# Group and mask columns of a neighborhood attention kernel, computed by GpSimd in the opening

## The chip, the core and the metric

The kernel runs on one core of a Trainium2 chip. The metric is device time in microseconds (us). Before the change, three runs took 326.32, 326.91 and 329.77 us, median 326.91. The engines are TensorE (PE in the profile, its weight loads PEld), VectorE (DVE), ScalarE (ACT), GpSimd (POOL) and SyncE (SP), which here only issues transfers.

## What is computed

A dilated neighborhood attention with one head on an image of 224 x 224 pixels and 192 channels. Each query attends to 7 x 7 keys, two pixels apart in both directions, in a window that is pushed inwards at the borders.

```python
qkv = x @ wqkv
q, k, v = qkv[..., :C], qkv[..., C:2 * C], qkv[..., 2 * C:]
r0 = clip(arange(H) - 6, 0, H - 13)
c0 = clip(arange(W) - 6, 0, W - 13)
ri = r0[:, None] + arange(7) * 2
ci = c0[:, None] + arange(7) * 2
...
logits = einsum('bnc,bnkc->bnk', q, k[nidx]) * C ** -0.5
p = softmax(logits, axis=-1)
o = einsum('bnk,bnkc->bnc', p, v[nidx]) @ wo
```

All arrays are bfloat16; `nidx` are the positions `ri * W + ci`.

## The kernel before

**Tiles and steps.** Since the dilation is 2, rows and columns of each parity are independent. The kernel works in 28 steps, each a row parity `rc` and a block `j` of 8 query rows of that parity, in an order written out by hand in `seq` (L508). A step has seven score groups (`s_group`, L397): per key tile `n` of 8 columns and column parity `cc`, two matmuls (L411 and L412) give the scores of 128 keys with up to 112 queries in PSUM, and ScalarE's Exp (L415) puts them into `p_sb`. The projections are folded into the weights: the query side `g = (scale * Wq Wk^T) x` is made by `g_piece` (L335) and `edge_item` (L287) from the transposed image `xt`, and the values are the plain image rows, with `Wv Wo` folded into `WP` (L265). `y_unit` (L417) multiplies `p_sb` with the values, `o_mm` (L440) applies `WP`, and `o_out` (L460) divides by the sum.

**The buffers that matter.** `XA` and `XB` hold the keys, `GA` and `GB` the query side. They have 192 channels in two parts; in `XB` and `GB` 64 of the 128 partitions are not needed for channels, and hold one-hot rows of the key's column and row (`onehots`, L191) against mask columns and mask rows (`masks`, L202): so the matmul L412 adds -30000 where a key lies outside the query's window. The mask columns are a copy of `cmE` (L187, written by VectorE from an iota of GpSimd); they are the same for all groups. There are six groups of `GB` buffers (`gorder`, L129), for row parity, block parity and border; `masks(eng, gi)` fills group `gi`, for both column parities unless one is named. `XN[rc]` holds the values: 14 tiles of 448 columns, of which the first 64 are the pattern `grp` (L155), written by `grp_copy` (L208) in two instructions (128x896, L209, and 128x64, L211), and 384 are loaded from the image (L104 and L110).

**What sets the order.** The schedule is manual: each engine works through its instructions in program order, and waits are put in where data depend on each other. What happens in the first two steps beside the score groups is written by hand in the table `early` (L532), by the number of the score group; later steps follow rules in the loop (L552). Masks of group 0 are written in the opening by VectorE (L214, L263), those of group 2 in entry 0 of `early`, of group 1 in entries 6 and 12, of groups 4, 3 and 5 in steps 2, 3 and 8 (L610). `grp_copy(0)` runs on ScalarE in the opening (L261), `grp_copy(1)` on ScalarE in entry 12 (L543).

**Queues.** SP issues the transposing loads of `xt` (L92), its half of the first value loads (L117) and the weights. GpSimd's program in the opening is: iotas (L134), three small memsets (L171 to L173), then the copy `gate` (L217), which reads one element of the second block of `xt` and so holds GpSimd until that part has landed; then seven value loads of `XN[0]` (L218), two copies of the one-hots by DMA (L195, in step 0), a second `gate` on `wo_hi` (L564), and the value loads of `XN[1]` and of the later steps (L104). Each transfer that GpSimd issues takes about 0.6 us of its time (L104: 595 ns).

Of the kernel before, what the change touches and what calls it, by code (L numbers as in the profile page):

```python
# [27 lines left out]
def kernel(  # L28
# [7 lines left out]
    nc = tc.nc  # L36
# [31 lines left out]
    GA, GB = {}, {}  # L68
# [7 lines left out]
    CROW = (slice(64, 96), slice(0, 32))  # L76
# [52 lines left out]
    gorder = [(0, 0, 1), (1, 0, 0), (0, 1, 0), (1, 1, 0), (0, 0, 0), (1, (NJ - 1) % 2, 1)]  # L129
# [49 lines left out]
    cmE = const.tile([128, S, BR], BF, name="cmE")  # L179
# [11 lines left out]
    def onehots(eng, cc, rc):  # L191
        c_, r_ = CROW[cc], RROW[cc]
        if rc == 1:
            both = slice(min(c_.start, r_.start), max(c_.stop, r_.stop))
            eng.dma_start(out=XB[cc][1][both], in_=XB[cc][0][both])  # L195
            return
        eng.tensor_copy(out=XB[cc][rc][c_].rearrange("p n (r c) -> p n r c", c=KC),
                        in_=t_c[c_].rearrange("p (n c) -> p n c", c=KC).unsqueeze(2).to_broadcast([32, NK, SLOTS, KC]))
        eng.tensor_copy(out=XB[cc][rc][r_],
                        in_=rowT[r_].rearrange("p r c -> p (r c)").unsqueeze(1).to_broadcast([32, NK, 128]))  # L200

    def masks(eng, gi, ccs=(0, 1)):  # L202
        for cc in ccs:
            g = GB[gorder[gi] + (cc,)]
            eng.tensor_copy(out=g[CROW[cc]], in_=cmE[CROW[cc]])
            eng.tensor_copy(out=g[RROW[cc]], in_=rm[RROW[cc], gi, :].unsqueeze(1).to_broadcast([32, S, BR]))

    def grp_copy(eng, rc):  # L208
        eng(out=XN[rc][:, 0:NK * XP].rearrange("p (n c) -> p n c", c=XP)[:, :, 0:64],  # L209
            in_=grp[:].unsqueeze(1).to_broadcast([128, NK, 64]))  # L210
        eng(out=XN[rc][:, NK * XP:], in_=grp[:])  # L211

    onehots(nc.vector, 0, 0)
    masks(nc.vector, 0, (0,))  # L214

    gate = const.tile([1, 1], BF, name="gate")
    nc.gpsimd.tensor_copy(out=gate[:], in_=xt[1][0:1, 0, 4, 0:1])  # L217
    load_both(nc.gpsimd, 0, (13, 11, 9, 7, 5, 3, 1))  # L218
# [29 lines left out]
    for nm, c, rows, o0, d0 in (("lo", 0, None, 0, 0), ("hi", 128, slice(0, 64), 128, 0), ("olo", -64, slice(64, 128), 0, 64), ("ohi", 64, None, 0, 0)):  # L248
# [7 lines left out]
        for dst, src in outs:  # L256
            if own:
                nc.vector.tensor_single_scalar(out=dst, in_=src, scalar=scale, op=ALU.mult)
            else:
                nc.scalar.mul(dst, src, scale)  # L260
    grp_copy(nc.scalar.copy, 0)  # L261
    onehots(nc.vector, 1, 0)
    masks(nc.vector, 0, (1,))  # L263

    def fold_wo():  # L265
# [113 lines left out]
    def slots(cc, n):  # L379

        lo, hi = KC * n, KC * n + QW
        if cc == 0:
            return [(lo, min(hi, S))]
        lo = max(lo, HALO)
        return [(lo, hi)] if hi <= S else [(lo, S), (0, hi - S)]
# [31 lines left out]
    def y_unit(st, cc, h, kt, eng, fill=0):  # L417
        h0, h1 = HS[h]
        kp = slice(0, 64 if st.first else 128)
        y = ps_y.tile([128, 512], F32, name="y", tag="y")  # L420
        for _ in range(fill):
            nc.tensor.matmul(y[:, 0:128], lhsT=ident[:], rhs=ident[:], start=True, stop=True)
        first = True
        for n in range(NK):
            if not any(max(lo, h0) < min(hi, h1) for lo, hi in slots(cc, n)):
                continue
            for (lo, hi, p, off) in st.p[(cc, n)]:
                a_, b_ = max(lo, h0), min(hi, h1)
                if a_ >= b_:
                    continue  # L430
                d = XP * n + ((128, 0), (256, 384))[cc][kt]
                nc.tensor.matmul(y[:, BR * (a_ - h0):BR * (b_ - h0)], lhsT=XN[st.rc][kp, d:d + 128],  # L432
                                 rhs=p[kp, off + BR * (a_ - lo):off + BR * (b_ - lo)],
                                 start=first, stop=True, skip_group_check=True)
                first = False
        i0, i1 = h0 // NO, h1 // NO
        o = st.ysb[cc][:, kt, :, :].rearrange("p n (i r) -> p i n r", r=BR)[:, i0:i1]
        eng(out=o, in_=y[:, 0:BR * (h1 - h0)].rearrange("p (i n r) -> p i n r", n=NO, r=BR))  # L438

    def o_mm(st, ns, ccs=(0, 1), home=None):  # L440

        if home is None:
            po = ps_go.tile([128, 4, 256], F32, name="po", tag="go")
        else:
            po = home[0].tile([128, 2, 256], F32, name="po" + home[1], tag=home[1])
        k = 0
        for n in ns:
            for cc in ccs:
                for kt in range(2):
                    nc.tensor.matmul(po[:, k, 0:C + 1], lhsT=st.ysb[cc][:, kt, n, :], rhs=WP[:, cc, kt, 0:C + 1],  # L450
                                     start=(kt == 0), stop=(kt == 1))
                k += 1
        rs = work.tile([128, 4, 1], F32, name="rs", tag="rs", bufs=4)
        nc.vector.reciprocal(out=rs[:, 0:k], in_=po[:, 0:k, C:C + 1])  # L454
        if st.o is None:
            st.o = work.tile([128, 2 * NO, C], BF, name="o_sb", tag="o_sb", bufs=4)
        t0, step = 2 * ns[0] + ccs[0], 3 - len(ccs)
        return po, rs, k, st.o[:, t0:t0 + step * (k - 1) + 1:step, :]

    def o_out(po, rs, k, o, act=False):  # L460
        if act:
            for i in range(k):
                nc.scalar.activation(out=o[:, i], in_=po[:, i, 0:C], func=ACTF.Copy, scale=rs[:, i])
            return
        nc.vector.tensor_tensor(out=o, in0=po[:, 0:k, 0:C], in1=rs[:, 0:k].to_broadcast([128, k, C]), op=ALU.mult)  # L465
# [46 lines left out]
    steps = []  # L512
# [13 lines left out]
    def run_y(now):  # L526
# [4 lines left out]

    early = {  # L532
        0: (lambda: masks(nc.vector, 2, (0,)), lambda: g_piece(0, 0, 2), lambda: key_copy(1, 0, 0, nc.scalar.copy, nc.vector.tensor_copy), lambda: key_copy(0, 0, 1, nc.vector.tensor_copy, nc.vector.tensor_copy), lambda: rest(nc.vector.tensor_copy), lambda: edge_item(0), lambda: masks(nc.vector, 2, (1,)),),
        2: (lambda: edge_copies(0, 0, nc.vector), lambda: g_piece(0, 1, 0),),
        3: (lambda: key_copy(0, 1, 1, nc.scalar.copy, nc.scalar.copy), lambda: g_piece(0, 1, 1, mid=nc.vector.tensor_copy, mid2=nc.vector.tensor_copy),),
# [4 lines left out]
        9: (lambda: y_unit(steps[0], 1, 0, 1, nc.scalar.copy), lambda: y_unit(steps[0], 1, 0, 0, nc.vector.tensor_copy),),  # L540
        10: (lambda: key_copy(1, 1, 1, nc.vector.tensor_copy, nc.vector.tensor_copy), lambda: fold_wo(), lambda: edge_copies(1, 0, nc.vector),),
        11: (lambda: o_out(*o_mm(steps[0], PIECES[0])), lambda: o_out(*o_mm(steps[0], PIECES[1])), lambda: y_unit(steps[1], 0, 0, 1, nc.scalar.copy), lambda: y_unit(steps[1], 0, 0, 0, nc.vector.tensor_copy),),
        12: (lambda: grp_copy(nc.scalar.copy, 1), lambda: masks(nc.vector, 1, (1,)), lambda: o_out(*o_mm(steps[0], PIECES[2])), lambda: y_unit(steps[1], 1, 1, 0, nc.scalar.copy),),  # L543
        13: (lambda: o_out(*o_mm(steps[0], PIECES[3])), lambda: y_unit(steps[1], 1, 1, 1, nc.scalar.copy),),
        14: (lambda: y_unit(steps[1], 1, 0, 1, nc.scalar.copy), lambda: y_unit(steps[1], 0, 1, 1, nc.vector.tensor_copy),),
        15: (lambda: y_unit(steps[1], 1, 0, 0, nc.vector.tensor_copy),),
# [4 lines left out]
    PIECES = ((0, 1), (2, 3), (4, 5), (6,))  # L551
# [129 lines left out]
```

## Time and profile before

| | us |
|---|---|
| median of three runs | 326.91 |
| profiled execution | 325.78 |
| its span, first to last instruction | 323.8 |
| TensorE busy | 306.1 (95%) |
| VectorE busy | 267.6 (83%) |
| ScalarE busy | 251.0 (78%) |
| GpSimd busy | 216.0 (67%) |

The mean granted TensorE clock is 0.993 of full speed. The profile is one execution, 325.78 us, which is 1.98 us more than its span. In a timeline a row gives the start in us, the duration, engine, line, operation, what is written from what, and the shape; in brackets stands the idle time of the engine before it and what ended that. In a group of instructions the two numbers after the bar are the busy time in us and the mean of one in ns. In a table of stretches the busy time of TensorE, its weight loads, VectorE, ScalarE and GpSimd follow each other.

### The profile page before, as it was taken

The numbers are of one execution on the slowest core, as the hardware profiler recorded it, in microseconds if no ns is written. First come the engines' busy times: TensorE is split into PE (matmuls) and PEld (weight loads), VectorE is DVE, ScalarE is ACT, GpSimd is POOL, SyncE is SP. The second block draws the span as 40 slices with busy tenths as digits, with TensorE's granted clock in tenths as the row PEclk, the third lists the DMA queues.
The fourth block names the chain that finished last, engine by engine and source line by source line (L and its number), as shares of the span: only waits on it lengthen the run. The fifth ranks groups of instructions, "written<-read, shape, count | busy, mean of one in ns | idle before, by whom it ended". The sixth has DMA issues, their size and how long they took to land.

```text
span 323.8 us, 12228 instructions
## 1 busy us (share of the span) xinstructions
PE 306.1 (95%) x4988; PEld 269.8 (83%) x4988; DVE 267.6 (83%) x533; ACT 251.0 (78%) x519; POOL 216.0 (67%) x445
## 2 busy tenths in 40 slices
PE   7689999998989999999999999999999999999981
PEld 6467987888879888988899888988899888988980
DVE  8968899987878989888988889888988898887771
ACT  5688767886868887878888798878787887888652
POOL 2144888797877766786667767679678786863053
PEclk9999999999999999999999999999999999999997
DMA  8999799999999999999998999899989943654233
GB/s 167 166 263 168 185 171 237 162 236 219 181 226 223 229 199 157 237 196 214 189 183 216 213 188 163 224 204 224 177 197 217 194 117 113 166 153 112 45 106 109
DMA packets 106109, 59.47 MB, mean 184 GB/s; under 512 B 92712, under 2 KB 100031, under 8 KB 106054
## 3 DMA queue, kind: packets, MB, share of 16 engines
q1 hardware_dynamic: 89270, 40.43, 64.6%
q0 software_dynamic: 16576, 18.13, 22.5%
q8 instruction: 39, 0.64, 0.9%
q10 hardware_dynamic: 208, 0.15, 0.2%
q14 instruction: 16, 0.13, 0.1%
HBM read 19.59 MB, written 19.27 MB: 120 GB/s over the span
## 4 chain that ended last, share of the span: by engine, by line
PE 54%; DMA 20%; DVE 7%; SPq 6%; POOL 5%; issue 4%; ACT 2%; POOLq 0%; DVEq 0%; ACTq 0%
DMA xn<-in_x_dram 16%; PE y L432 15%; PE po L450 12%; PE pg L354 10%; PE s_ps L411 7%; PE s_ps L412 7%; SPq L92 4%; DMA out_dram<-o_sb 4%; DVE o_sb L465 4%; POOL xn L104 3%; PE pg L362 3%; DVE ysb L438 2%; SPq L110 1%; POOL out_dram L608 1%; ACT ysb L438 1%
## 5 line engine op out<-in xcount | busy, mean ns | idle before, releaser
L104 POOL DMA_DIRECT2D xn<-in_x_dram x316 | 178.6, 595 | 58.6 <-DMA xn<-in_x_dram 24.9
L415 ACT ACTIVATE p_sb<-s_ps 128x448 bf16<-128x448 f32 (+3 forms) x196 | 105.4, 539 | 21.3 <-PE s_ps L412 20.7
L432 PE MATMUL y<-p_sb,xn 128*128 128x112 bf16 (+5 forms) x1736 | 107.3, 207 | 1.6 <-DMA xn<-in_x_dram 1.3
L432 PEld LDWEIGHTS <-xn 128*128 128x128 bf16 (+1 forms) x1736 | 94.8, 97 | 13.9 <-issue 5.4
L411 PE MATMUL s_ps<-ga,xa 128*128 128x112 bf16 (+4 forms) x812 | 98.1, 210 | 1.4 <-DVE xa L278 0.8
L412 PE MATMUL s_ps<-gb,xb 128*128 128x112 bf16 (+4 forms) x812 | 97.8, 210 | 0.1
L438 ACT CAST ysb<-y 128x504 bf16<-128x504 f32 (+1 forms) x137 | 71.6, 543 | 33.4 <-PE y L432 31.8
L465 DVE TENSOR_TENSOR o_sb<-po,rs 128x768 bf16<-128x768 f32 x109 | 93.6, 859 | 4.7
L450 PE MATMUL po<-WP,ysb 128*128 128x193 bf16 x770 | 82.6, 247 | 1.0 <-DVE ysb L438 0.5
L412 PEld LDWEIGHTS <-xb 128*128 128x128 bf16 (+1 forms) x812 | 75.8, 98 | 0.9 <-issue 0.6
L411 PEld LDWEIGHTS <-xa 128*128 128x128 bf16 (+1 forms) x812 | 72.6, 98 | 2.2 <-DVE xa L278 1.0
L450 PEld LDWEIGHTS <-ysb 128*128 128x128 bf16 x784 | 62.7, 98 | 2.9 <-ACT ysb L438 1.1
L354 PE MATMUL pg<-xt,wz 128*128 128x327 bf16 (+3 forms) x336 | 51.2, 288 | 1.7 <-DMA xt<-in_x_dram 1.6
L438 DVE CAST ysb<-y 128x392 bf16<-128x392 f32 (+1 forms) x87 | 51.7, 596 | 0.6 <-PE y L432 0.2
L454 DVE RECIPROCAL rs<-po 128x4 f32<-128x4 f32 x110 | 19.4, 177 | 23.2 <-PE po L450 21.7
L368 DVE CAST gb<-pg 64x872 bf16<-64x872 f32 x27 | 28.6, 1057 | 5.0 <-PE pg L362 3.6
L354 PEld LDWEIGHTS <-wz 128*128 128x128 bf16 x336 | 24.4, 98 | 9.8 <-DMA xt<-in_x_dram 1.9
L366 ACT CAST ga<-pg 128x872 bf16<-128x872 f32 x28 | 24.8, 884 | 8.4 <-PE pg L354 8.3
L371 DVE CAST gb<-pg 64x848 bf16<-64x848 f32 x28 | 29.2, 1044 | 0.4
L278 ACT COPY xa<-xt 128x896 bf16<-128x896 bf16 x28 | 26.3, 939 | 0.0
L376 ACT CAST ga<-pg 128x848 bf16<-128x848 f32 x28 | 24.2, 864 | 0.5 <-PE pg L354 0.3
L280 DVE COPY xb<-xt 64x896 bf16<-64x896 bf16 x54 | 21.4, 396 | 0.8
(93 smaller groups left out, 182.4 us busy)
## 6 DMA issues: line engine op xcount, KB each, us to landing
out_dram<-o_sb SPq DMA_DIRECT2D x25, 630.0 KB
xn<-in_x_dram POOLq DMA_DIRECT2D x316, 48.0 KB, 4.5
xn<-in_x_dram SPq DMA_DIRECT2D x38, 48.0 KB
xn<-in_x_dram SPq DMA_DIRECT2D x12, 96.0 KB
out_dram<-o_sb POOLq DMA_DIRECT2D x12, 78.8 KB, 4.2
xt<-in_x_dram SPq DMA_TRANSPOSE x56
out_dram<-o_sb SPq DMA_DIRECT2D x50, 9.0 KB
xn<-in_x_dram POOLq DMA_DIRECT2D x7, 96.0 KB, 3.9
```

The costliest lines, as they stand in the source:

```text
L104: eng.dma_start(out=XN[rc][p0:p0 + 64, XP * n + 64:XP * (n + 1)], in_=xp[r0:r0 + 15:2, KC * n:KC * (n + 1), :])
L278: ea(out=XA[rc][:, cc, :, k0:k0 + 64].rearrange("p n (r c) -> p r n c", c=KC), in_=t[:, 2 * cc, rc:16:2, :].rearrange(v, c=KC))
L354: nc.tensor.matmul(pg[:, a_:b_, 0:nq], lhsT=AW[w], rhs=xt[b][:, k, la:la + 2 * (b_ - a_ - 1) + 1:2, q0:q0 + nq], start=(a_ == ra if kind = ...
L368: mid(out=Bt[0][0:64, 3:S, :], in_=pg[0:64, :, 0:nq].rearrange(v))
L371: mid(out=Bt[1][64:128, HALO:S, :], in_=pg[64:128, :, 3:nq].rearrange(v))
L411: nc.tensor.matmul(o, lhsT=XA[rc][:, cc, n, 0:kn], rhs=a[:, lo:hi, :].rearrange(f), start=True, stop=False)
L412: nc.tensor.matmul(o, lhsT=XB[cc][rc][:, n, 0:kn], rhs=b_[:, lo:hi, :].rearrange(f), start=False, stop=True)
L415: nc.scalar.activation(out=p[0:kn, 0:off], in_=s_ps[0:kn, 0:off], func=ACTF.Exp)
L432: nc.tensor.matmul(y[:, BR * (a_ - h0):BR * (b_ - h0)], lhsT=XN[st.rc][kp, d:d + 128], rhs=p[kp, off + BR * (a_ - lo):off + BR * (b_ - lo) ...
L438: eng(out=o, in_=y[:, 0:BR * (h1 - h0)].rearrange("p (i n r) -> p i n r", n=NO, r=BR))
L450: nc.tensor.matmul(po[:, k, 0:C + 1], lhsT=st.ysb[cc][:, kt, n, :], rhs=WP[:, cc, kt, 0:C + 1], start=(kt == 0), stop=(kt == 1))
L465: nc.vector.tensor_tensor(out=o, in0=po[:, 0:k, 0:C], in1=rs[:, 0:k].to_broadcast([128, k, C]), op=ALU.mult)
```

## The change

GpSimd fills the group columns of both value buffers and the mask columns of groups 2, 1 and 4, ahead of its first `gate` and so of its first loads. ScalarE no longer does the group columns, VectorE no longer the mask columns of these three groups; it keeps the mask rows of all groups and the mask columns of groups 0, 3 and 5. GpSimd's order is: `grp_copy(0)`, masks of group 2 (two instructions of 32x896), of group 1 (two), `grp_copy(1)`, masks of group 4 (two). The computation is the same.

```diff
+    def mask_cols(gi):
+        for cc in range(2):
+            nc.gpsimd.tensor_copy(out=GB[gorder[gi] + (cc,)][CROW[cc]], in_=cmE[CROW[cc]])
+
     def masks(eng, gi, ccs=(0, 1)):
         for cc in ccs:
             g = GB[gorder[gi] + (cc,)]
-            eng.tensor_copy(out=g[CROW[cc]], in_=cmE[CROW[cc]])
+            if gi in (0, 3, 5):
+                eng.tensor_copy(out=g[CROW[cc]], in_=cmE[CROW[cc]])
             eng.tensor_copy(out=g[RROW[cc]], in_=rm[RROW[cc], gi, :].unsqueeze(1).to_broadcast([32, S, BR]))
...
     masks(nc.vector, 0, (0,))
 
+    grp_copy(nc.gpsimd.tensor_copy, 0)
+    mask_cols(2)
+    mask_cols(1)
+    grp_copy(nc.gpsimd.tensor_copy, 1)
+    mask_cols(4)
     gate = const.tile([1, 1], BF, name="gate")
     nc.gpsimd.tensor_copy(out=gate[:], in_=xt[1][0:1, 0, 4, 0:1])
     load_both(nc.gpsimd, 0, (13, 11, 9, 7, 5, 3, 1))
...
-    grp_copy(nc.scalar.copy, 0)
     onehots(nc.vector, 1, 0)
...
-        12: (lambda: grp_copy(nc.scalar.copy, 1), lambda: masks(nc.vector, 1, (1,)), ...
+        12: (lambda: masks(nc.vector, 1, (1,)), ...
```

More of the change, by code (lines that the diff above doesn't have):

```diff
@@ L542 @@
         11: (lambda: o_out(*o_mm(steps[0], PIECES[0])), lambda: o_out(*o_mm(steps[0], PIECES[1])), lambda: y_unit(steps[1], 0, 0, 1, nc.scalar.copy), lambda: y_unit(steps[1], 0, 0, 0, nc.vector.tensor_copy),),
-        12: (lambda: grp_copy(nc.scalar.copy, 1), lambda: masks(nc.vector, 1, (1,)), lambda: o_out(*o_mm(steps[0], PIECES[2])), lambda: y_unit(steps[1], 1, 1, 0, nc.scalar.copy),),
+        12: (lambda: masks(nc.vector, 1, (1,)), lambda: o_out(*o_mm(steps[0], PIECES[2])), lambda: y_unit(steps[1], 1, 1, 0, nc.scalar.copy),),
         13: (lambda: o_out(*o_mm(steps[0], PIECES[3])), lambda: y_unit(steps[1], 1, 1, 1, nc.scalar.copy),),
```

## Prediction

> **What bounds the kernel now.** I read the page first: the span and how full TensorE is.
>
> ```profile
> span 323.8 us, 12228 instructions
> PE 306.1 (95%) x4988; PEld 269.8 (83%) x4988; DVE 267.6 (83%) x533; ACT 251.0 (78%) x519; POOL 216.0 (67%) x445
> ...
> PE   7689999998989999999999999999999999999981
> ```
>
> TensorE is busy for 306.1 of 323.8 us, and its row of tenths shows 8 or 9 from the third slice to the last but one. Elsewhere the kernel gets shorter only if a gap of TensorE closes, and longer if one opens that no later wait takes up. So the next view is the timeline of TensorE, of which I show the waits that decide here (in brackets: idle time before the row, and what ended it).
>
> ```profile
> 10.88 0.22 PE L411 MATMUL s_ps<-ga,xa 128*64 128x64 bf16 x1 [0.81 <-DVE xa L278]
> ...
> 16.45 0.55 PE L354 MATMUL pg<-xt,wz 128*128 128x436 bf16 x2 [1.06 <-DMA xt<-in_x_dram]
> ```
>
> ```profile
> 43.04 0.83 PE L450 MATMUL po<-WP,ysb 128*128 128x193 bf16 x8 [0.25 <-ACT ga L376]
> 50.39 0.55 PE L354 MATMUL pg<-xt,m 128*128 128x436 bf16 x3 [0.18 <-DVE o_sb L465]
> ```
>
> ```profile
> 76.24 0.35 PE L296 MATMUL pe<-xt,wz 128*128 128x48 bf16 x6 [0.86 <-DMA xt<-in_x_dram]
> ```
>
> ```profile
> 90.37 0.32 PE L432 MATMUL y<-p_sb,xn 128*128 128x112 bf16 x3 [1.30 <-DMA xn<-in_x_dram]
> ```
>
> The first score matmul waits for VectorE's key copy; at 16.45, 76.24 and 90.37 the wait is for transfers. The waits for ACT and DVE between 35 and 60 are small.
>
> Then the timelines of the three engines that the change touches, GpSimd first:
>
> ```profile
> 14.90 0.19 POOL L217 COPY gate<-xt 1x1 bf16<-1x1 bf16 x1 [11.86 <-DMA xt<-in_x_dram]
> 15.04 3.87 POOL L110 DMA_DIRECT2D xn<-in_x_dram  x7
> 18.84 1.21 POOL L195 DMA_DIRECT2D xb<-xb  x2
> 28.36 0.18 POOL L564 COPY gate<-wo_hi 1x1 bf16<-1x1 bf16 x1 [8.31 <-DMA wo_hi<-in_wo_dram]
> ```
>
> GpSimd stands idle for 11.86 us up to 14.90, which means from 3.04, and again for 8.31 us up to 28.36.
>
> ```profile
> 4.26 0.63 DVE L187 COPY cmE<-cm 128x896 bf16<-128x896 bf16 x1
> ...
> 5.24 0.62 DVE L197 COPY xb<-t_c 32x1792 bf16<-32x1792 bf16 x1
> ...
> 6.53 0.38 DVE L205 COPY gb<-cmE 32x896 bf16<-32x896 bf16 x1
> ...
> 7.33 0.36 DVE L258 TENSOR_SCALAR wz<-pry 128x192 bf16<-128x192 f32 x1
> ...
> 7.96 0.36 DVE L258 TENSOR_SCALAR wz<-pry 128x192 bf16<-128x192 f32 x1
> ...
> 10.43 0.39 DVE L278 COPY xa<-xt 128x896 bf16<-128x896 bf16 x1
> ...
> 18.56 1.06 DVE L368 CAST gb<-pg 64x872 bf16<-64x872 f32 x1 [2.27 <-PE pg L362]
> ```
>
> VectorE has no gap in this stretch until 2.27 us before 18.56: whatever slows one of its instructions before 10.43 comes out at the key copy, and so at TensorE's 10.88.
>
> **The change, part by part.**
>
> *Taken from ScalarE.* By instructions on the value buffers:
>
> ```profile
> L209 ACT COPY xn<-grp x2: 930/930/930, 5.9 to 35.3; 128x896 bf16<-128x896 bf16 x2
> L211 ACT COPY xn<-grp x2: 245/246/248, 6.8 to 36.2; 128x64 bf16<-128x64 bf16 x2
> ```
>
> ```profile
> 8.69 0.89 ACT L366 CAST ga<-pg 128x872 bf16<-128x872 f32 x1 [1.67 <-PE pg L354]
> ```
>
> ```profile
> 35.00:40.00 5.00, 4.98 (x93) 4.45 (x91) 4.77 (x13) 4.57 (x10) 4.03 (x8) 1.00 0.63 162
> ```
>
> ScalarE loses 2 x (0.93 + 0.25) = 2.36 us. The first pair lies ahead of 1.67 us of idle time: worth 0. The second, at 35.3, lies where TensorE (first busy column) has 4.98 of 5.00 us: worth 0 there, and at most the 0.25 us of 43.04 later.
>
> *Taken from VectorE.* Six mask-column copies:
>
> ```profile
> L205 DVE COPY gb<-cmE 32x896 bf16<-32x896 bf16 x12 | 4.8, 400 | 0.3
> ```
>
> 6 x 0.40 = 2.4 us less on VectorE. None of the six stands ahead of the first key copy (groups 2, 1 and 4 are filled after it; group 0 stays on VectorE), so none helps 10.88. Two lie before the 2.27 us gap, which would only get longer; the others can close at most the 0.18 us of 50.39. I take 0 for both removals; the end for the range is a gain of 0.25 + 0.18 = 0.43 us.
>
> *Added to GpSimd.* Two group copies of 128x896, two tails of 128x64, six mask columns of 32x896: eight of 896 elements, two of 64. No row has so long a copy on GpSimd. The nearest are its edge copies:
>
> ```profile
> L332 POOL COPY gb<-ge 64x48 bf16<-64x48 bf16 x16 | 3.7, 229 | 0.9
> ...
> L332 POOL COPY gb<-ge 64x18 bf16<-64x18 bf16 x9 | 1.9, 209 | 0.5
> ```
>
> From 18 to 48 elements 20 ns, of which one delayed copy (below) accounts for 7: 13/30 = 0.43 ns an element. So 0.209 + 878 x 0.00043 = 0.59 us for 896 elements, an extrapolation. Ends: 0.40, what VectorE takes for the same copy, and 0.93, what ScalarE takes for the group copy. I take 0.59, since it alone comes from GpSimd's own rows; a 64-element tail is 0.23. Sum 8 x 0.59 + 2 x 0.23 = 5.2 us, in an idle stretch of 11.86.
>
> [...]
>
> *What GpSimd's copies do to VectorE.* Two pairs of rows where the two overlap:
>
> ```profile
> 241.39 0.33 POOL L332 COPY gb<-ge 64x48 bf16<-64x48 bf16 x1
> ```
>
> ```profile
> 241.24 0.39 DVE L280 COPY xb<-xt 64x896 bf16<-64x896 bf16 x1
> ```
>
> ```profile
> 136.42 0.21 POOL L332 COPY gb<-ge 64x18 bf16<-64x18 bf16 x1
> ```
>
> ```profile
> 136.46 0.42 DVE L280 COPY xb<-xt 64x896 bf16<-64x896 bf16 x1
> ```
>
> ```profile
> L280 DVE COPY xb<-xt x54: 374/390/454, 10.7 to 293.4; 64x896 bf16<-64x896 bf16 x54
> ```
>
> In the first pair GpSimd starts 0.15 us after VectorE and takes 0.33 us instead of 0.22; it ends 0.09 us after VectorE's end (241.72 against 241.63). In the second, VectorE starts 0.04 us after GpSimd and takes 0.42 instead of the median 0.39; it ends 0.25 us after GpSimd's end. So a copy that comes second does some 0.13 us of its own start beside the first, and the rest after it: they exclude each other. Casts from PSUM beside GpSimd's copies show nothing of the kind. Where the engines take turns, each GpSimd copy costs VectorE 0.59 - 0.13 - 0.14 = 0.32 us.
>
> How many meet? cmE is ready at 4.26 + 0.63 = 4.89, so the first group copy runs alone, against VectorE's small instructions from 3.04 on: one charge. After 4.89 VectorE has six SBUF-to-SBUF instructions up to 7.33 (L188, L189, L197, L199, L205, L206), against which the four masks of groups 2 and 1, the second group copy and its tail take turns: five charges, the tail none. Then come the three PSUM instructions (L258), 7.33 to 8.32: about 1.0 us in which the last two masks (1.2 us) run nearly free, say 0.1 us. Sum: 6 x 0.32 + 0.1 = 2.0 us. The key copy ends at 12.8 and the first score matmul starts near 12.9 instead of 10.88. By the ends: at 0.93 a copy 0.66 a charge and seven of them, 4.6 us; at 0.40 six of 0.13, 0.8 us; and 0 if GpSimd always yields.
>
> GpSimd itself would end near 10.5 (8.32 + 2.0): 4.4 us ahead of the gate at 14.90, so the seven loads (L110), the two copies of xb (L195) and all behind them on its queue don't move. If that cover went, they would move with it, up to the 8.31 us of idle time at 28.36, which protects only what follows that. SP's queue isn't touched. The readers of the new writes come long after: the value buffer's group columns and group 2's masks past 22 us.
>
> *What becomes of 2.0 us.* The wait of 1.06 at 16.45 is for a transpose that SP issued on its own, so TensorE arrives later and waits less: 0.9 us left. Then TensorE runs nearly full until 76.24 and 90.37, where it waits 0.86 + 1.30 = 2.16 us for transfers. If those come at the old times, all 0.9 is gone; if GpSimd's issues move with TensorE, nothing is. The chain of waits and GpSimd's timeline:
>
> ```profile
> 42.11 5.86 DMA xn<-in_x_dram
> ```
>
> ```profile
> 108.04 3.88 POOL L104 DMA_DIRECT2D xn<-in_x_dram  x7 [0.40 <-PE y L432]
> ```
>
> The chain passes at 42.11 from TensorE into an xn transfer, so there the loads do hang on TensorE; from then on the gaps of GpSimd are ended by earlier transfers, and the first of them that TensorE ends is at 108.04. Between the two I take half: +0.4 us. The ends are 0 and 0.9.
>
> Sum: 0 for the removals, 0 on GpSimd, +0.4 through VectorE. The profiled execution took 325.78 us (323.8 of span and 1.98 around it): 326.2. The runs' median stands 1.13 above that execution, so against it the forecast is 327.3 us, no difference that can be told.
>
> **The rivals.**
>
> *GpSimd yields, or the delay is wholly absorbed.* For it: the transfers' waits of 2.16 us; the pair at 241 shows GpSimd as the one that waits. Against: the pair at 136. Time: the old median less the small gaps, 326.91 - 0.43 = 326.5 us. To be faster by over 1% (3.27 us, about what a measurement of this kernel can tell) it would need 2.8 us more from TensorE's waits, which before 35 us are set by transfers and key copies that the change doesn't hasten.
>
> *The long copies are long (the other side).* Place: VectorE between 4.89 and 10.43. If a copy takes 0.93, the delay of 4.6 loses only 1.06 at 16.45, and if the later waits move along, the end is 326.91 + 3.5 = 330.4 us, slower by 1.1%. It decides from 7 x (c - 0.27) - 1.06 = 3.27, c = 0.89 us a copy. For it: ScalarE needs 0.93 for as many elements. Against: the slope of GpSimd's rows. GpSimd would then end near 13.5, still ahead of 14.90.
>
> *TensorE falls back to its slow rate.* The opening's fillers show two rates:
>
> ```profile
> 1.66 1.67 PE L225 MATMUL fill<-ident 128*128 128x128 bf16 x14 [1.66 <-DVE ident L152]
> ...
> 5.78 0.50 PE L225 MATMUL fill<-ident 128*128 128x128 bf16 x6
> ...
> 7.19 0.83 PE L347 MATMUL pg<-ident 128*128 128x128 bf16 x12
> ```
>
> Fourteen in 1.67 us at first, twelve of the same in 0.83 later. The wait of 0.81 before 10.88 becomes 2.8 us; if that brings back the slow phase, which lasted up to 4.1 us (1.66 to 5.78), at half the rate up to 2.05 us are lost: 327.3 + 2.0 = 329.3 us. Against: waits of 1.06 and 1.30 us leave no trace. [...]
>
> **How the numbers follow.** My forecast 0.50; GpSimd yields or full absorption 0.22; long copies 0.20; slow rate 0.08. The likeliest gives 327.3. The range starts at 325.4: 326.5 of the first rival, and about a microsecond of the runs' scatter, which reaches from 326.32 to 329.77 about 326.91; it ends at 331.5, a microsecond over the long copies, which leaves out copies over a microsecond long. Faster by over 1%: 0.05, out of the first rival, for what its bound overlooks. Slower by over 1%: 0.20, most of the long copies and a little of the slow rate. Within 1%: 0.75.
>
> **What would show it.** GpSimd's timeline: ten copies from 3.04 to about 10.5, those of 896 elements near 0.59 us where nothing holds them, the gate still at 14.9. VectorE: L197, L199, L205 and L206 lengthened by some 0.3 us each up to L258, and none after; L278 near 12.4. TensorE: first score matmul near 12.9, the 1.06 us at 16.45 gone or nearly, y at 25 us up to a microsecond late, smaller waits near 76 and 90. The forecast is wrong if the copies take 0.9 us or more, if VectorE's rows don't lengthen, or if the gate moves past 15.

## The result, and the profile after

| | before | after |
|---|---|---|
| median (six runs each) | 325.97 | 329.58 |
| profiled execution | 325.78 | 329.41 |
| its span | 323.8 | 327.4 |
| mean granted TensorE clock | 0.993 | 0.979 |

The ratio is 1.0134 with a 95% interval of 1.0094 to 1.0173: slower by 1.3%. The forecast was 327.3 us, a difference that can't be told; the time lies inside its range, 2.3 us above the likeliest value and 0.8 us below the long-copies rival. As a change it is +3.6 us by the two medians of six runs (+4.4 by the ratio), where the forecast's sum had +0.4 and the long-copies rival +3.5.

In the changed kernel the lines are shifted: L204 is `mask_cols`, L210 and L211 are VectorE's mask columns and rows (L205, L206), L214 and L216 are `grp_copy`, L227 is the gate, L268 was L258, L287 and L289 are the key copies (L278, L280), L363 and L371 are `g_piece`, L420 and L421 are the score matmuls (L411, L412). The page first, with its clock row in tenths:

```profile
span 327.4 us, 12230 instructions
PE 308.5 (94%) x4988; PEld 271.6 (83%) x4988; DVE 270.8 (83%) x527; ACT 249.8 (76%) x515; POOL 225.5 (69%) x455
...
PE   7389999999999999999999999999999999999981
...
PEclk9759999999999999999999999999999999999997
```

The loss arises in the opening: TensorE's second slice, 8.2 to 16.4 us, falls from 6 tenths to 3, and the clock's second and third slices from 9 to 7 and 5. GpSimd's timeline of the changed kernel:

```profile
3.10 0.94 POOL L214 COPY xn<-grp 128x896 bf16<-128x896 bf16 x1
3.99 0.23 POOL L216 COPY xn<-grp 128x64 bf16<-128x64 bf16 x1
5.69 4.56 POOL L204 COPY gb<-cmE 32x896 bf16<-32x896 bf16 x4 [1.47 <-DVE i_r L188]
10.20 1.08 POOL L214 COPY xn<-grp 128x896 bf16<-128x896 bf16 x1
11.23 0.23 POOL L216 COPY xn<-grp 128x64 bf16<-128x64 bf16 x1
11.52 2.19 POOL L204 COPY gb<-cmE 32x896 bf16<-32x896 bf16 x2
13.73 0.50 POOL L227 COPY gate<-xt 1x1 bf16<-1x1 bf16 x1
```

The first copy, which meets only small instructions, takes 0.94 us, the other group copy 1.08, and the masks 4.56 / 4 = 1.14 and 2.19 / 2 = 1.10 each. GpSimd ends at 13.7, and the gate follows at once. VectorE's timeline beside it:

```profile
3.29 0.82 DVE L182 TENSOR_SCALAR t_c<-i_c 128x112 bf16<-128x112 int32 x1
...
5.91 1.24 DVE L197 COPY xb<-t_c 32x1792 bf16<-32x1792 bf16 x1
7.16 1.25 DVE L199 COPY xb<-rowT 32x1792 bf16<-32x1792 bf16 x1
8.45 1.01 DVE L210 COPY gb<-cmE 32x896 bf16<-32x896 bf16 x1
...
9.47 1.02 DVE L211 COPY gb<-rm 32x896 bf16<-32x896 bf16 x1
10.51 0.36 DVE L268 TENSOR_SCALAR wz<-pry 128x192 bf16<-128x192 f32 x1
...
11.53 1.40 DVE L197 COPY xb<-t_c 32x1792 bf16<-32x1792 bf16 x1
12.94 1.25 DVE L199 COPY xb<-rowT 32x1792 bf16<-32x1792 bf16 x1
...
15.11 0.40 DVE L287 COPY xa<-xt 128x896 bf16<-128x896 bf16 x1
```

Four of the rows of before that belong to these, and that the prediction doesn't show:

```profile
3.29 0.22 DVE L182 TENSOR_SCALAR t_c<-i_c 128x112 bf16<-128x112 int32 x1
...
5.87 0.62 DVE L199 COPY xb<-rowT 32x1792 bf16<-32x1792 bf16 x1
...
6.93 0.39 DVE L206 COPY gb<-rm 32x896 bf16<-32x896 bf16 x1
...
8.35 0.62 DVE L197 COPY xb<-t_c 32x1792 bf16<-32x1792 bf16 x1
```

Each SBUF copy that meets one of GpSimd's takes 0.62 to 0.63 us longer than its row of before (0.62 to 1.24 and 1.25, 0.38 to 1.01, 0.39 to 1.02; the L197 at 11.53, which starts 0.01 us after a mask, 0.78; the small L182 at 3.29 went from 0.22 to 0.82). The PSUM instruction L268 keeps its 0.36. Seven rows lengthen, by 0.60 + 5 x 0.63 + 0.78 = 4.5 us, and the key copy stands at 15.11 instead of 10.43, 4.68 late. TensorE's timeline shows what this makes of it:

```profile
11.25 0.54 PE L363 MATMUL pg<-xt,m 128*128 128x327 bf16 x3 [2.32 <-DVE m L268]
11.72 0.57 PE L371 MATMUL pg<-xt,wz 128*64 128x327 bf16 x6
12.22 0.62 PE L235 MATMUL fill<-ident 128*128 128x128 bf16 x8
15.56 0.26 PE L420 MATMUL s_ps<-ga,xa 128*64 128x64 bf16 x1 [2.72 <-DVE xa L287]
...
16.62 1.59 PE L363 MATMUL pg<-xt,wz 128*128 128x318 bf16 x6
...
91.13 0.30 PE L441 MATMUL y<-p_sb,xn 128*128 128x112 bf16 x3 [0.46 <-DMA xn<-in_x_dram]
```

There are two waits, of 2.32 us for the folded weight `m` and of 2.72 for the key copy. Then the six matmuls at 16.62 take 1.59 us, where before they took this:

```profile
11.62 0.91 PE L354 MATMUL pg<-xt,wz 128*128 128x318 bf16 x6
```

The tables of stretches give the clock (the number behind the engines' columns), before and after:

```profile
10.00:15.00 5.00, 3.16 (x46) 2.31 (x45) 4.79 (x13) 3.09 (x6) 0.10 (x1) 1.00 1.11 159
15.00:20.00 5.00, 3.94 (x47) 2.48 (x45) 2.64 (x8) 3.89 (x10) 4.93 (x10) 1.00 1.07 261
20.00:25.00 5.00, 4.40 (x71) 3.46 (x71) 4.11 (x10) 4.96 (x9) 0.05 (x1) 1.00 1.14 246
```

```profile
10.00:15.00 5.00, 1.58 (x17) 0.93 (x17) 4.85 (x8) 0.88 (x1) 4.86 (x8) 0.80 1.11 203
15.00:20.00 5.00, 3.44 (x29) 2.26 (x30) 3.68 (x9) 2.20 (x3) 4.41 (x8) 0.50 0.98 235
20.00:25.00 5.00, 5.00 (x51) 3.43 (x50) 1.67 (x8) 3.44 (x9) 0.00 (x0) 0.67 1.11 236
```

A mean of 0.80, 0.50 and 0.67 comes from a granted clock of 0.5 from 13.04 to 23.28 us in the trace: 10.24 us, or three stretches of 3.41 us, the length of the shortest half-clock stretch of the traces (18.61 to 22.02 with a few wide fillers, below). In what follows, this is the half clock. When the matmuls of both traces are set side by side, one by one, TensorE is 4.68 us late at its first score matmul, 6.2 at 17.6 us of the time before, 6.0 at 25, 5.1 at 52 to 75, 4.2 at 77, 3.3 at 91, and 3.5 at the end.

### The profile page after: what moved, and what is told of

Its sections match the earlier page's. It is cut to its first block, busy times and chain, and to the rows that moved or that the text cites. A ratio compares the mean times of both kernels' runs of the same rounds, so it can differ in the third digit from the quotient of the medians.

```text
span 327.4 us, 12230 instructions
## 1 busy us (share of the span) xinstructions
PE 308.5 (94%) x4988; PEld 271.6 (83%) x4988; DVE 270.8 (83%) x527; ACT 249.8 (76%) x515; POOL 225.5 (69%) x455
## 4 chain that ended last, share of the span: by engine, by line
PE 67%; DMA 10%; DVE 9%; SPq 5%; ACT 3%; issue 3%; POOL 1%; POOLq 0%; DVEq 0%; ACTq 0%
PE y L441 18%; PE po L459 16%; PE pg L363 12%; PE s_ps L420 8%; PE s_ps L421 8%; DMA out_dram<-o_sb 6%; DVE o_sb L474 5%; DMA xn<-in_x_dram 4%; SPq L92 4%; PE pg L371 3%; DVE ysb L447 2%; PE pe L305 1%; SPq L110 1%; DVE rs L463 1%; ACT ysb L447 1%
## 5 line engine op out<-in xcount | busy, mean ns | idle before, releaser
L420 PE MATMUL s_ps<-ga,xa 128*128 128x112 bf16 (+4 forms) x812 | 99.1, 211 | 3.2 <-DVE xa L287 2.7
L421 PE MATMUL s_ps<-gb,xb 128*128 128x112 bf16 (+4 forms) x812 | 99.0, 211 | 0.0
L421 PEld LDWEIGHTS <-xb 128*128 128x128 bf16 (+1 forms) x812 | 76.7, 99 | 0.8 <-issue 0.4
L420 PEld LDWEIGHTS <-xa 128*128 128x128 bf16 (+1 forms) x812 | 73.5, 99 | 4.5 <-DVE xa L287 2.9
L363 PE MATMUL pg<-xt,wz 128*128 128x327 bf16 (+3 forms) x336 | 52.4, 293 | 0.5 <-DMA xt<-in_x_dram 0.4
L363 PEld LDWEIGHTS <-wz 128*128 128x128 bf16 x336 | 24.8, 99 | 8.8 <-DMA xt<-in_x_dram 0.6
L287 ACT COPY xa<-xt 128x896 bf16<-128x896 bf16 x28 | 26.3, 939 | 0.0
L289 DVE COPY xb<-xt 64x896 bf16<-64x896 bf16 x54 | 21.9, 406 | 0.8
```

What stands on the lines that cost most here:

```text
L287: ea(out=XA[rc][:, cc, :, k0:k0 + 64].rearrange("p n (r c) -> p r n c", c=KC), in_=t[:, 2 * cc, rc:16:2, :].rearrange(v, c=KC))
L363: nc.tensor.matmul(pg[:, a_:b_, 0:nq], lhsT=AW[w], rhs=xt[b][:, k, la:la + 2 * (b_ - a_ - 1) + 1:2, q0:q0 + nq], start=(a_ == ra if kind = ...
L420: nc.tensor.matmul(o, lhsT=XA[rc][:, cc, n, 0:kn], rhs=a[:, lo:hi, :].rearrange(f), start=True, stop=False)
L421: nc.tensor.matmul(o, lhsT=XB[cc][rc][:, n, 0:kn], rhs=b_[:, lo:hi, :].rearrange(f), start=False, stop=True)
```

## The experiments

The first theory was that VectorE's delay and the half clock are each worth part of the loss; the rivals were that only one of them counts, or that the relief of ScalarE and VectorE or an earlier gate matter. All ratios are to the kernel before on the same chip, with 95% intervals. "Late" is the start of the same matmul against the trace of before.

**The copies alone, without the relief.** Ten copies of the same shapes on GpSimd into an unused tile `dup`; ScalarE and VectorE keep all of their work.

```diff
+    dup = const.tile([128, S, BR], BF, name="dup")
...
+    dup_group()
+    dup_cols()
+    dup_cols()
+    dup_group()
+    dup_cols()
     gate = const.tile([1, 1], BF, name="gate")
```

> The kernel before, with the ten GpSimd copies of the change written to an unused tile ahead of the first gate; nothing is taken from VectorE or ScalarE. Theory (the loss comes from what GpSimd's copies do to VectorE): VectorE's SBUF copies up to the key copy lengthen by 0.63 us each as in the changed kernel, the clock falls, end +3.5 to +4.5 us; the part above the changed kernel's +3.5 is what the relief is worth. Rival (the loss comes from where the readers now wait, for GpSimd instead of VectorE and ScalarE): end within 0.5 us of before.

Measured: 330.16 us, ratio 1.0148 (1.0105 to 1.0191); the key copy at 14.84, TensorE's two waits 2.17 and 2.51 us, the half clock again for 10.24 us. The copies alone cost what the change costs. The relief would be the difference, 0.14%, well inside the intervals.

**Only the group columns moved.** `grp_copy(0)` and `grp_copy(1)` on GpSimd in the opening, all masks on VectorE.

```diff
+    grp_copy(nc.gpsimd.tensor_copy, 0)
+    grp_copy(nc.gpsimd.tensor_copy, 1)
     gate = const.tile([1, 1], BF, name="gate")
```

> The group columns alone on GpSimd (two copies of 128x896, two of 128x64), the masks as before on VectorE. Theory: two copies of 0.94 us meet VectorE's small instructions from 3.1 on, at 0.65 each: key copy 1.3 us late, of which 1.06 goes into the wait for the transpose at 16.45; clock full; end within 0.5 us of before. Rival (the prediction's price of 0.32 each): key copy 0.6 late, end the same. Second rival (each copy costs its share of the 3.5 us at the end): +0.8 us.

**Only the mask columns moved.**

```diff
+    mask_cols(2)
+    mask_cols(1)
+    mask_cols(4)
     gate = const.tile([1, 1], BF, name="gate")
```

> The mask columns of groups 2, 1 and 4 alone on GpSimd (six copies of 32x896), the group columns on ScalarE as before. Theory: five meet, at 0.63: key copy 3.2 us late. If the clock stays full, 2.1 us late at 25 and +0 to +1 us at the end; if it falls, 2 us more. Rival (loss in proportion to the copies): six of eight, +2.6 us whether or not the clock falls.

Measured: the group columns alone 324.56 us, ratio 0.9954 (0.9928 to 0.998), the masks alone 328.15 us, 1.0083 (1.0052 to 1.0114). So the change holds a part that helps by 0.5%, more than the half microsecond that the theory allowed, and one that harms, by 2.6 us between the medians (the theory had 2 to 3 us with a fallen clock; the rival's 2.6 fits as well). The timelines of GpSimd and TensorE with the group columns alone:

```profile
4.17 0.92 POOL L209 COPY xn<-grp 128x896 bf16<-128x896 bf16 x1
5.04 0.23 POOL L211 COPY xn<-grp 128x64 bf16<-128x64 bf16 x1
13.75 0.30 POOL L219 COPY gate<-xt 1x1 bf16<-1x1 bf16 x1 [8.48 <-DMA xt<-in_x_dram]
```

```profile
12.25 0.22 PE L412 MATMUL s_ps<-ga,xa 128*64 128x64 bf16 x1 [1.22 <-DVE xa L279]
...
12.99 0.91 PE L355 MATMUL pg<-xt,wz 128*128 128x318 bf16 x6
```

Here both long copies come before 5.3 us, against VectorE's smallest instructions: two charges, the key copy 1.37 us late (11.80), and the six matmuls at 12.99 keep 0.91 us. With the masks alone:

```profile
11.45 0.54 PE L362 MATMUL pg<-xt,m 128*128 128x327 bf16 x3 [2.40 <-DVE m L266]
14.26 0.26 PE L419 MATMUL s_ps<-ga,xa 128*64 128x64 bf16 x1 [1.22 <-DVE xa L286]
```

The key copy is 3.4 us late (13.81), and the clock is half from 13.45 to 23.69.

**The clock kept up with many fillers.** Fillers are matmuls with the unit matrix whose result nobody reads; they only keep TensorE busy. Narrow ones have 128 columns, wide ones 512. The changed kernel with 36 more narrow fillers ahead of the second query piece and 48 instead of 8 ahead of the first score group.

```diff
+    filler(36)
...
-    filler(8)
+    filler(48)
```

> The changed kernel, with 36 more filler matmuls ahead of the second query piece and 48 instead of 8 ahead of the first score group, so that TensorE works through its two waits of 2.3 and 2.7 us. Theory (exclusion delays VectorE by 4.7 us, and the slow TensorE clock from 13.0 to 23.3 us adds some 2.5): key copy still near 15.1, clock full throughout, TensorE some 3.6 us late at 25 us instead of 6.1, and the end some 1 us after the kernel before, 2.5 us ahead of the changed kernel. Rival (the waits on VectorE and ScalarE alone carry the loss, the slow clock only fills them): clock full, but lateness and end as in the changed kernel, +3.5 us.

Measured: 329.14 us, ratio 1.0128 (1.0083 to 1.0174). In its stretches:

```profile
10.00:15.00 5.00, 4.59 (x71) 3.73 (x68) 4.85 (x8) 0.88 (x1) 4.30 (x7) 1.00 1.17 188
15.00:20.00 5.00, 3.10 (x44) 2.33 (x45) 4.22 (x11) 2.66 (x5) 4.69 (x9) 1.00 1.11 243
```

The clock is whole, the key copy as late as ever (15.03), and TensorE is 3.8 us late at 25 instead of 6.0, 3.1 instead of 5.1 at 75: the mechanism up to there. But in its profiled execution (331.25, the longest of its four) TensorE then waited 2.20 us for a transfer at 92, a half-clock stretch followed, and it ended 5.5 late. The ratio shows no gain that can be told.

**The clock kept up with a few wide fillers.** The same purpose with 20 more instructions of 512 columns instead of 76 of 128.

```diff
+    wide(9)
...
+    wide(11)
```

> The changed kernel, with TensorE's two waits filled by 20 wide matmuls (512 columns) instead of the 76 narrow ones of the earlier run, so that far fewer instructions are added and their fetch isn't drawn ahead. Theory (the slow clock costs 2.5 us at 25 us, and of that some reaches the end if the transfers let it): clock full, key copy near 15.1, TensorE 3.6 us late at 25; the end between 1 and 2.5 us after before, 1 to 2.5 ahead of the changed kernel. Rival (the value loads, which from 42 us on wait for TensorE, lose the rest anyway, as in the run with narrow fillers): end as there, +3.5 us.

Measured: 328.33 us, ratio 1.0106 (1.0054 to 1.0158), all four executions between 328.24 and 328.52; one half-clock stretch, 18.61 to 22.02, instead of three; 5.1 late at 25, 2.4 at the end of this trace. By the ratio the end is 3.4 us after before, which is the rival's 3.5 and not the theory's 1 to 2.5. It is 0.3% under the changed kernel, and the intervals overlap.

**The same work later.** The masks of groups 1 and 4 and the second group copy on GpSimd behind its first loads and the two `xb` transfers; the rest as before.

```diff
+            mask_cols(1)
+            grp_copy(nc.gpsimd.tensor_copy, 1)
+            mask_cols(4)
```

> Part of the change, moved: the masks of groups 1 and 4 and the second group copy on GpSimd, but behind its first loads and its two xb transfers (some 20 to 26 us, where it stood idle for 8.3 us); the first group copy stays on ScalarE and group 2's masks on VectorE. Theory (what a GpSimd copy costs depends on whether VectorE's SBUF copies stand beside it): there VectorE mostly reads PSUM, so at most the copies at 20.7, 22.7, 23.7 and 25.2 are held up, one to two of them on TensorE's path; TensorE at most 1 us late at 30 us, clock full, loads on GpSimd's queue not later, end between -1 and +0.5 us against before. Rival (each copy costs the same wherever it stands): five copies, three fifths of the changed kernel's loss, +2 us.

Measured: 325.91 against 326.56 us, 0.9978 (0.9943 to 1.0014). The copies still take 0.92 to 1.03 us each, at 20.1 to 25.4, where most of VectorE's work is casts from PSUM (L376 beside a mask 1.04 us, as before); two of its SBUF copies lengthen, by 0.40 and 0.30 us (L211 0.79, L285 0.69), and TensorE is at most 1.0 late up to 75: no difference that can be told, and not the rival's +2 us. It is the place that makes the copies dear.

**The helpful part with late masks.** Both group copies in the opening, masks of groups 1 and 4 behind the loads.

```diff
+    grp_copy(nc.gpsimd.tensor_copy, 0)
+    grp_copy(nc.gpsimd.tensor_copy, 1)
...
+            mask_cols(1)
+            mask_cols(4)
```

> A version meant to be the best: both group copies on GpSimd in the opening, ahead of cmE, as in the run with the group columns alone; the masks of groups 1 and 4 on GpSimd behind its first loads; group 2's masks on VectorE. Theory: key copy 1.3 us late as there, of which the wait for the transpose takes 1.06; later VectorE is relieved of four copies where TensorE is full; end 0.5 to 1.5 us ahead of before, like the group columns alone. Rival (relief of VectorE and ScalarE is worth what it takes off them): a microsecond better than the group columns alone.

Measured: 324.59 us, 0.996 (0.9929 to 0.9991), the same as with the group columns alone: taking four mask columns from VectorE adds nothing that can be told.

**Half the length, first try.** All ten copies as int32 pairs, so half the elements for the same bytes.

```diff
+            nc.gpsimd.tensor_copy(out=GB[gorder[gi] + (cc,)][CROW[cc]].bitcast(I32), in_=cmE[CROW[cc]].bitcast(I32))
...
+        xi, gi32 = XN[rc][:].bitcast(I32), grp[:].bitcast(I32)
```

> The changed kernel with GpSimd's ten copies over pairs of bf16 as 32-bit integers: the same bytes, half the elements. Theory (GpSimd pays by the element, and VectorE's delay is that of each copy less some 0.3 us of overlap): a copy alone takes some 0.56 us instead of 0.94, the key copy ends some 2 us late instead of 4.7 (this is the size that the prediction worked with), TensorE's waits stay under 1.6 us each and the clock full; end 0 to +1 us against before. Rival (GpSimd pays by the byte): 0.94 us a copy and +3.5 us as in the changed kernel.

Measured: 344.34 us, 1.0553 (1.05 to 1.0605). It went another way than either theory: with the value buffer written as int32 (the next run, with the masks alone as int32, doesn't show this) the first copy waited until 22.80, behind SP's value loads and weights, and the gate and GpSimd's loads with it; TensorE then stood for values.

```profile
22.80 0.56 POOL L215 COPY xn<-grp 128x448 int32<-128x448 int32 x1 [19.76 <-DMA wo_hi<-in_wo_dram]
23.30 0.20 POOL L217 COPY xn<-grp 128x32 int32<-128x32 int32 x1
```

```profile
39.52 1.29 PE L442 MATMUL y<-p_sb,xn 64*128 64x56 bf16 x14 [16.99 <-DMA xn<-in_x_dram]
```

It says nothing of the meeting with VectorE. It does give the price of an element, (0.56 - 0.20) / 416 = 0.87 ns, against (0.94 - 0.23) / 832 = 0.85 ns for bfloat16: for these two widths GpSimd pays by the element and not by the byte. And it shows what the cover of the gate was worth: with the gate at 35.22 and GpSimd's loads 20 us later than before, TensorE stands for 17 us.

**Half the length, masks alone as pairs.** The change with its six mask copies as int32, the group copies as bfloat16.

```diff
+            nc.gpsimd.tensor_copy(out=GB[gorder[gi] + (cc,)][CROW[cc]].bitcast(I32), in_=cmE[CROW[cc]].bitcast(I32))
```

> The changed kernel with GpSimd's six mask copies over pairs of bf16 as 32-bit integers, group copies as changed. Theory (GpSimd pays 0.85 ns an element whatever its width, VectorE's charge is the copy less some 0.3 us): mask copies of 0.55 us at 0.25 each, group copies as before at 0.65; key copy some 2.5 us late instead of 4.7, near the 2.0 of the prediction. TensorE's waits near 1.4 us each; if the clock stays full 1.4 us late at 25, and the end between -0.5 and +1 us; if a window of 3.4 us falls to half, 1 us more. Rival (a copy's charge is fixed, whatever its length): 4.7 us and +3.5.

Measured: 326.89 us, 1.0075 (1.0044 to 1.0106).

```profile
5.68 3.07 POOL L204 COPY gb<-cmE 32x448 int32<-32x448 int32 x4 [1.46 <-DVE i_r L188]
...
10.03 1.16 POOL L204 COPY gb<-cmE 32x448 int32<-32x448 int32 x2
```

A mask takes 3.07 / 4 = 0.77 us where it takes turns with VectorE and 0.58 beside the PSUM instructions; the key copy is 2.7 us late (13.13) instead of 4.7. So VectorE's delay goes with the length of GpSimd's copies; a charge that each copy makes whatever its length would have left it at 4.7. The end missed the theory's +1 us, or +2 with one stretch of half clock: in the trace two stretches were at half clock (13.44 to 20.26), and TensorE was 3.7 late at 25.

**A control.** The kernel before, again.

> The kernel before, unchanged, as a control and for a second profile of it. Same time within 0.3%. If transfers land by chance a microsecond earlier or later (theory for the gate at 14.9 us, which came at 13.7 to 14.5 in the other kernels, and for the waits at 76 and 90 us), this profile differs from the first in those places by as much; rival: the gate and those waits are the same to 0.2 us, so that the other kernels' earlier gate is a consequence of what they change.

Measured: 326.1 against 326.56 us, 0.9992 (0.9953 to 1.0031). The gate stands at 15.04 in its trace (14.90 in the first), while the waits near 76 to 91 us differ from one execution to the next (0.88, 0.61 and 0.84 instead of 0.86 and 1.30): the gate's time can be compared between kernels, a single one of these waits can't.

**Is it the earlier gate?** The gate comes at 13.3 to 14.4 us in the kernels with copies or other fillers in the opening (but for the one that waited for the weights), at 14.9 to 15.0 in the kernel before, its control and the kernel with late copies. The transfers of before, 12 to 14 us, and of the kernel with the group columns alone, 14 to 16 us (packets, MB, share of 16 engines' time):

```profile
q8 instruction: 1, 0.02, 4.9%
```

```profile
q8 instruction: 1, 0.02, 3.6%
```

Each is one load of 16 KB of instructions: 4.9% of 16 x 2 us is 1.6 us, at 12.5 in the kernel before, ahead of the transposed part that the gate waits for; with the group columns alone it comes at 14.6, behind that part. The load isn't all that counts: with the copies alone it comes at 17.8 and the gate still waits for its part until 14.4, and with many fillers it comes at 10.8 and the gate opens at 14.3. To move the load without any copy, 20 narrow fillers of the kernel before were replaced by 5 wide ones (those inside `g_piece` too):

```diff
-    g_piece(0, 0, 0, fill=12)
+    g_piece(0, 0, 0, fill=3)
...
-    filler(8)
+    wide(2)
```

> The kernel before, nothing moved to GpSimd; only 20 of its narrow filler matmuls (128 columns) ahead of the first score group are replaced by five wide ones (512 columns) that take as long. Theory (a fetch of 16 KB of instructions, in step with TensorE's instruction count, stands at 12.5 us in front of the transpose that GpSimd's gate waits for; in the run with the group columns alone it came at 14.6, behind it): with 30 TensorE instructions fewer it moves to some 14 us, the gate opens near 13.6 instead of 14.9, the value loads go out 1.2 us earlier, the waits for transfers near 76 and 90 us shrink, and the end is 0.5 to 1.5 us ahead of before, like the group columns alone. Rival (there the relief of ScalarE made the gain): gate earlier or not, the end as before within 0.3 us.

Measured: 324.31 against 324.49 us, 1.000 (0.9971 to 1.0029). The load moved to 16.0 (the theory had some 14) and the gate to 13.31, as the theory had it; the end stayed, as the rival had it. But there the load stood ahead of the next transpose:

```profile
18.62 0.94 ACT L283 COPY xa<-xt 128x896 bf16<-128x896 bf16 x1 [1.20 <-DMA xt<-in_x_dram]
```

ScalarE waited 1.20 us, TensorE 1.86 after it (at 21.12), and it was 1.9 us late at 25 and 0.3 early at the end. Here the earlier gate gave nothing to the end, while TensorE was made late by other means; whether it is what helps the group columns this run doesn't settle.

**The helpful part with the clock kept up.** Of the ten executions with the group columns alone, the five with a mean clock of 0.991 or more have a median of 323.4 us, the three with 0.984 or less 325.3. So, in that kernel, six of the eight fillers ahead of the first score group became wide ones.

```diff
-    filler(8)
+    filler(2)
+    wide(6)
```

> The kernel with the group columns alone on GpSimd, with six of the eight fillers ahead of the first score group replaced by wide ones (512 columns), so that TensorE's wait of 1.22 us at the first score matmul is filled to about 0.4; the number of TensorE's instructions is the same. Of the ten executions of the kernel with the group columns alone, five have a mean granted clock of 0.991 or more (median 323.4 us) and three of 0.984 or less (median 325.3). If the half-clock windows of the opening cause that difference, then the clock is 0.991 or more in nearly all executions here, their median is near 323.5 and the ratio to the kernel before about 0.992 to 0.994. The rival: the clock is a companion and not the cause, or the loss is given back at the later transfer waits; then the clock is higher and the ratio stays at 0.995 to 0.996. If the windows don't depend on the wait, executions at 0.984 and less are seen as before.

Measured: 323.77 us, ratio 0.9936 (0.9905 to 0.9968), and all twelve executions have a clock of 0.991 or more. TensorE's timeline:

```profile
12.24 0.22 PE L417 MATMUL s_ps<-ga,xa 128*64 128x64 bf16 x1 [0.19 <-DVE xa L284]
```

TensorE's wait of 1.22 us at the first score matmul has become 0.19. This is the lowest ratio here. That the fillers do away with the low-clock executions is shown (twelve of twelve, against five of ten; the runs were on different chips); that they beat the group columns alone (0.9954) isn't, since the intervals overlap. The waits of TensorE for transfers, grouped, first in the kernel before and then here:

```profile
PE pg L354 <- DMA xt<-in_x_dram: 1.6, 2, 1.1
PE y L432 <- DMA xn<-in_x_dram: 1.3, 1, 1.3
...
PE pe L296 <- DMA xt<-in_x_dram: 0.9, 1, 0.9
```

```profile
PE pg L360 <- DMA xt<-in_x_dram: 1.1, 2, 0.8
```

The waits of 1.3 and 0.9 us at 90 and 76 are gone in this execution, and TensorE goes from 0.7 late at 75 to 1.7 early at 91.

## Why the prediction was right and wrong, point by point

**The removals, taken as 0: right, as far as can be told.** Copies without relief give 1.0148, with relief 1.0134; late masks add nothing that can be told to the group columns. These intervals are too wide to test a bound of 0.43 us. The group columns alone are faster by 0.46%, some 1.5 us, which is more than that bound; I argue, without a run that isolates it, that this comes from the transfers at 76 and 90, which come sooner after the earlier gate, and not from ScalarE. Their trace speaks for it: between 35 and 52 us, where ScalarE had its second copy before, TensorE gains 0.1, but it goes from 0.6 late at 75 to 1.1 early at 91. The two other kernels with the group columns in the opening are 1.4 and 1.7 early at 91; the control and the kernel with late copies, whose gates stand at 15.0, are 0.5 and 0.4 late there.

**A copy of 896 elements, taken as 0.59 us: the step that failed.** The slope of 0.43 ns an element came from rows of 18 and 48 elements, and it holds among those: undisturbed they take 0.21 and 0.22 us, and the tail of 64 elements takes the 0.23 that was forecast. From 64 to 896 elements the slope is 0.85 (0.23 and 0.94 us). Why the first few dozen elements cost less is open. The copy takes 0.94, which was the upper end of the range, the row of ScalarE for the same copy; by the prediction's own sign, copies of 0.9 us or more, its likeliest case is refuted, and only the range held. The sum of 5.2 us became 8 x 0.94 + 2 x 0.23 = 8.0 undisturbed.

**GpSimd and VectorE exclude each other: right in kind, and mis-sized with the copy.** 0.94 - 0.13 - 0.14 = 0.67 was the charge to expect of a copy of this length, 0.62 to 0.63 was measured in five rows, 0.60 against a smaller instruction, and the PSUM instructions stayed at 0.36. The count was right at its upper end: seven charges, 4.5 us, where the bound said seven and 4.6. The key copy was 4.68 late, not 2.0, and halving the masks' length cut it to 2.7.

**The gate unmoved at 14.9: wrong, on the good side.** GpSimd ended at 13.7, near the 13.5 of the upper end, but the gate went there with it: its part had landed by then, and the 16 KB of instructions, which came at 19.0, no longer stood before it. That this is the reason is argued from the run with fewer fillers; the copies alone and the many fillers don't fit it well. What this is worth in the changed kernel isn't known: GpSimd later waits 5.00 us for TensorE, up to the loads at 43.98, so the head start isn't kept.

**The wait of 1.06 at 16.45 absorbs: right.** It is gone from the trace.

**Half of the later waits absorbs: near.** Of the 0.86 + 1.30 us, TensorE won back 5.14 - 4.16 = 0.98 at 76 and 4.16 - 3.32 = 0.84 near 90, 1.8 in all, and 1.0 more in smaller waits between 25 and 52 us. But with 6.0 late at 25, this leaves 3.3, not 0.4. This is one execution, and the control shows that these waits vary.

**The slow-clock rival, given 0.08: it happened.** From 4.68 - 1.06 = 3.6 expected at 25 us to 6.0 found, 2.4 us are left over for the half clock, a little over the 2.05 of the rival; the kernel with many fillers, whose clock stayed whole, is 3.8 late there. How much of the 2.4 us reaches the end isn't settled: by the two kernels with fillers 0 to 0.3% of the time, with intervals that overlap. In the prediction it was an alternative to the long copies, while it is their consequence: the same copies make the two waits of 2.32 and 2.72 us. Where the first ends, TensorE works for 1.6 us (11.25 to 12.84), and between 9.63 and 13.04, the 3.41 us before the clock fell, it stood for the rest: 1.58 of 3.41 us of work, 0.46. The fall is no accident of where these stretches lie: any 3.41 us that start between 6.5 and 14.1 hold less than 0.58 of work, and all six executions have a mean clock of 0.975 to 0.980. That waits of 1.06 and 1.30 us leave no trace, which the prediction had against this rival, says nothing of these two.

**The rivals weighed together.** The long copies were given 0.20 and 330.4 us; they came, from 0.89 us a copy on, as that part said, and the time was 329.58. Its sum had 3.5 us of loss from the copies alone; in fact 3.6 us of copies and 2.4 of clock were reduced by 2.5 up to the end. Its time was close partly by luck, since two omissions, the clock and the absorption, offset each other. The forecast itself had given "slower by over 1%" a chance of 0.20.

## What to carry to other kernels

An extrapolation over a factor of twenty in size, from rows of 0.21 and 0.22 us, which 30 elements set only 0.01 us apart, is a guess; if a row of another engine for the same size gives the other end, the forecast belongs nearer to that end. Before work goes to an idle engine, ask not only whether it has the time, but which instructions of VectorE stand there: ahead of a key copy a copy on GpSimd cost VectorE 0.63 us, beside a PSUM cast nothing that shows (1.04 us with and without it). And move parts on their own: of this change the group columns alone are worth half a per cent, and the masks, which come when VectorE has SBUF copies, lose more than that.

## What the runs showed beyond this

For the two widths that ran, GpSimd's copy paid by the element and not by the byte: 896 bfloat16 0.94 us, the same bytes as 448 int32 0.56 us. The clock fell in other kernels with even smaller waits, one 3.41-us stretch at 13.87 in the kernel with late copies, where TensorE's only waits in the ten microseconds ahead were 0.54 and 0.95 us; so a wait that does nothing in one kernel may cost a stretch in another.

The traces show more of when the clock falls. Its changes in the opening lie whole stretches of 3.41 us after the moment at which the full clock first comes, and that moment is another in each execution (4.96 to 7.65 us). Of these stretches at full clock up to 25 us, it fell after each of the ten that held 0.45 to 0.57 of matmul work, and after none that held 0.60 or more; two with 0.51 and 0.54, each the first at full clock, had no fall behind them, nor did a later one with 0.49 (75.3 to 78.7 with late copies), so this is no exact rule. The group columns alone and the helpful part with late masks have the same two waits, 1.22 and 0.95 us: in the trace of the second the first wait and most of the other lie in one stretch (11.06 to 14.48, 1.57 us of work), and the clock fell; in the trace of the first a border at 13.05 parts them (2.11 and 2.47 us of work), and it didn't. With the six wide fillers every 3.41 us of the opening hold 0.63 or more, wherever the borders lie, which fits its twelve executions without a low clock.

And instructions of TensorE shift the loading of 16 KB of code: it starts when TensorE has begun 93 to 100 matmuls in thirteen of the fourteen traces (115 in the one with fewer fillers), at 10.8 to 19.0 us, and takes 0.9 to 1.8 us. In the kernel before, the transposed part behind it landed at 14.9 us, with fewer fillers at 13.3.
